# Local and downsampled attention with a gated MLP on one core: the opening's order planned anew

## The chip, the core and the metric

The kernel runs on one core of one Trainium2 chip. The core has a matrix engine (PE, with its weight loads beside it), a vector engine (DVE), a scalar engine (ACT), GpSimd (POOL) and a queue engine (SP). Each takes its instructions in order. Transfers are issued from SP, ACT and POOL. The metric is the device time of one execution in microseconds (us); less is better.

## The reference

Eight batches, eight heads, 576 positions, 64 numbers a head. The attention output is a coarse attention over means of four positions, repeated four times, plus a local attention in which a position sees those at a distance under four. The result, as 4608 tokens of 512, goes through an RMS norm and a gated MLP of width 1536.

```python
q_d, k_d, v_d = (t.reshape(B, H, S // 4, 4, D).mean(axis=3) for t in (q, k, v))
out_up = np.repeat(sm_attn(q_d, k_d, v_d), 4, axis=2)
mask = np.abs(pos[:, None] - pos[None, :]) < 4
scores = np.where(mask, scale * np.matmul(q, k.transpose(0, 1, 3, 2)), -1e9)
x = out_up + np.matmul(softmax(scores), v)         # then tokens x 512
xn = x / np.sqrt(np.mean(x * x, axis=-1, keepdims=True) + 1e-06) * rms_g
g, val = xn @ w_gate, xn @ w_val
return (g * (1.0 / (1.0 + np.exp(-g))) * val) @ w_out
```

## The kernel before

The tokens are cut into 18 chunks of 256. A chunk's MLP (class `Forward`) has six steps `n`: a gate and a value product of the first layer (`first`, L1388; x and weights are each split into a high and a low half, three matmuls for one product), the gating on ACT and DVE (`tanh`, `gate`, `product`, `high`, L1396 to L1410), the low half of the gated product (`low`, L1413, on DVE or POOL), and the second layer (`second`, L1427), which runs a step behind.

The x of a chunk comes from local attention. From chunk 2 on, class `Attention` makes it on DVE (scores L917 and L921, sums of values L980), with a part of the value products on ACT (L963) and, for chunks 2 and 3, on POOL (L970); then come the squares, the mean across partitions (L1010), an inverse root by three Newton steps (L718 to L731), the norm, and a turn of x on PE (L1033) into the halves `xh` and `xl` (L1037, L1041). Chunks 0 and 1 are made by class `Early` with matmuls instead: four scores for each of two units (`score`, L1166 for the band mask and L1168 for the products, on 64 rows each), their maxima (L1181), a scaling of the maxima (`less`, L1185), exponentials (L1192), an inverse sum (L1198, L1199), turns (L1227, L1238), the values (L1258), the coarse result spread over four positions (`spread`, L1265), a copy (`keep`, L703 is the line of all copies), squares (L1278) and a turn (L1303).

The coarse attention (class `Coarse`) runs for a batch and a pair of heads: scores (L593), maxima (L603), their scaling (L608), exponentials (L613), turns (L623), values (L638), an inverse sum (L644, L647), a scaled result (L656) that goes out to memory (L659). Its sums over four positions are made for batch 0 on DVE (L473, L481; class `OpeningSums`, which also puts the queries in order on ACT, L467) and later by accumulating transfers from POOL (L417).

The weights arrive as 64-bit floats and are decoded in 20 pieces (`load_weight`, `decode`): a scaling on ACT (L315), the last bits on POOL (L325), a join on DVE (L332), a high half on ACT (L339) and a low half on DVE (L346, L344). The first layer's halves are multiplied by the norm's gain `g_sb`, which `load_small` fetches from POOL's queue (L1535) with the edge masks (L1534).

Until chunk 3 the order of all this is written out by a planner at build time (class `Plan`). Each step is a task with an engine (or a choice of two), a cost in us, a due time and the buffers that it takes and uses; a transfer has a size times `MB` us, and a table `RANK` holds one due time for every task. The planner goes through time, gives each free engine the task with the earliest due time of those that can start first, and calls it; the instructions stand on each engine in that order (`manual_schedule`) as long as a task's planned start is before `due[FIRST] + 10`. After that the same calls are made, and the framework's own scheduler orders them; from chunk 3 a hand-written interleaving (`steps`) follows.

`heat` fills PE's planned idle time with matmuls on constants (L504), so that the clock stays up. In the opening they go into a spare PSUM tile of the pool `ps_o`, which has two buffers; the two units of chunk 0 use that pool for their values, and the spare is closed as the second of them begins (`value`).

Of the kernel before, what the change touches and what calls it, by code (L numbers as in the profile page):

```python
# [19 lines left out]
P = 128  # L20
# [31 lines left out]
WARM_AT = 6.5  # L52
WARM_SHARE = 0.95
WARM_LEAST = 0.4
MB = 3.1
# [72 lines left out]
class Plan:  # L128
# [9 lines left out]
    def add(self, engine, cost, fn, due, after=(), with_=(), allocs=(), uses=(), not_before=0.0, dma=0.0, lag=0.0, hw=0, sw=0):  # L138
# [45 lines left out]
    def run(self, until=1e9):  # L184
        free, ready = self.free, self.ready
        while self.left:
# [19 lines left out]
            if s >= until:  # L206
                return
            cost = next(o for o in t.options if o[0] == e)[1]
            t.start = s
            self.idle, self.gap = (s - max(known, WARM_AT), s - max(free[e], WARM_AT)) if e == "PE" else (0.0, 0.0)  # L210
# [20 lines left out]
def attn_moe_kernel(  # L231
# [25 lines left out]
    ps_o = ctx.enter_context(tc.tile_pool(name="ps_o", bufs=2, space=PSUM))  # L257
# [99 lines left out]
    def load_second(f, m):  # L357
# [9 lines left out]
        "up_t": 2, "xh0": 1, "xh1": 1, "xl0": 1, "xl1": 1, "sil": 2, "hs": 2, "o_sb": W_BUFS, "ps_h": 3, "ps_o": 2, "ps_a": 3,  # L367
# [60 lines left out]
    class OpeningSums:  # L428


        def __init__(self, b, half):
            self.b, self.half = b, half
            self.qk_buf, self.vs_buf, self.q_buf = buf("qk"), buf("vs"), buf("hs")
            self.got = task("SP", 0.4, self.load_qk, -100 + half, dma=1.18 * MB, hw=1)
# [1220 lines left out]
```

## Time and profile before

| | us |
|---|---|
| median of three runs | 1089.92 (1088.96 to 1090.8) |
| the profiled execution | 1089.94 |
| its span, first to last instruction | 1088.1 |
| PE busy | 1066.7 (98%) |
| PE weight load busy | 970.2 (89%) |
| DVE busy | 909.6 (84%) |
| ACT busy | 598.6 (55%) |
| POOL busy | 160.8 (15%) |
| first-layer matmuls (L1388), both forms | 632.6 + 482.5 |
| second-layer matmuls (L1427) | 327.1 |

Busy times of matmuls overlap, so that those of single groups add up to more than the engine's. A matmul of the filler counts as busy as well. A row of a group gives line, engine, operation, output and inputs by the program's names, shapes and count, then busy us and mean ns of one, then the idle time of the engine just before them and what ended most of it. A row of a timeline gives start, duration, engine, line and operation, and in brackets the idle time before it with what ended it. The releaser is inferred: where the engine named had long been done, it was another.

### The profile page before, as it was taken

The numbers are of one execution on the slowest core, as the hardware profiler recorded it, in microseconds if no ns is written. First come the engines' busy times: TensorE is split into PE (matmuls) and PEld (weight loads), VectorE is DVE, ScalarE is ACT, GpSimd is POOL, SyncE is SP. The second block draws the span as 40 slices with busy tenths as digits, with TensorE's granted clock in tenths as the row PEclk, the third lists the DMA queues.
The fourth block names the chain that finished last, engine by engine and source line by source line (L and its number), as shares of the span: only waits on it lengthen the run. The fifth ranks groups of instructions, "written<-read, shape, count | busy, mean of one in ns | idle before, by whom it ended". The sixth has DMA issues, their size and how long they took to land.

```text
span 1088.1 us, 21642 instructions
## 1 busy us (share of the span) xinstructions
PE 1066.7 (98%) x7983; PEld 970.2 (89%) x7983; DVE 909.6 (84%) x1554; ACT 598.6 (55%) x2029; POOL 160.8 (15%) x200
## 2 busy tenths in 40 slices
PE   7899999999999999999999999999999999999997
PEld 4569899899989999999999999999999999999996
DVE  7799999798969897979797979798998898986421
ACT  4686565737266565656564737383737373645111
POOL 6544564300210101010101010100000000000000
PEclk9899999999999999999999999999999999999999
DMA  9885657333654535353525253522221222210000
GB/s 292 274 237 167 182 134 155 77 91 86 132 102 117 118 99 102 107 106 87 126 85 128 68 130 86 132 77 82 63 86 54 79 78 74 80 40 20 1 20 20
DMA packets 79182, 114.09 MB, mean 105 GB/s; under 512 B 33038, under 2 KB 40406, under 8 KB 79076
## 3 DMA queue, kind: packets, MB, share of 16 engines
q1 hardware_dynamic: 48308, 88.40, 26.3%
q0 software_dynamic: 11680, 19.78, 11.6%
q10 hardware_dynamic: 19088, 4.53, 1.9%
q8 instruction: 62, 1.02, 0.4%
q14 instruction: 44, 0.36, 0.1%
HBM read 100.86 MB, written 11.80 MB: 104 GB/s over the span
## 4 chain that ended last, share of the span: by engine, by line
PE 85%; DVE 6%; DMA 3%; issue 2%; POOL 2%; ACT 1%; SPq 1%; DVEq 0%; POOLq 0%; ACTq 0%
PE ps_h L1388 51%; PE ps_o L1427 25%; PE ps_a L638 3%; DMA w<-in_w_val_dram 1%; PE ps_a L593 1%; PE ps_a L623 1%; DVE prod L917 1%; PE ps_a L1033 1%; DVE x_t L980 1%; DVE sc L921 1%; PE ps_a L1258 1%; DVE sil L1404 0%; POOL hs L1413 0%; DMA vs<-in_v_sum_dram 0%; DMA wo<-in_w_val_dram 0%
## 5 line engine op out<-in xcount | busy, mean ns | idle before, releaser
L1388 PE MATMUL ps_h<-xh,w 128*128 128x256 f32 x3456 | 632.6, 281 | 0.0
L1388 PEld LDWEIGHTS ps_h<-xh,w 128*128 128x128 f32 x3456 | 537.6, 188 | 9.7 <-issue 3.1
L1388 PE MATMUL ps_h<-xl,w 128*128 128x256 f32 x1728 | 482.5, 280 | 0.0
L1427 PE MATMUL ps_o<-wo,hs 128*128 128x512 f32 x1296 | 327.1, 396 | 4.2 <-POOL hs L1413 1.7
L1388 PEld LDWEIGHTS ps_h<-xl,w 128*128 128x128 f32 x1728 | 325.2, 188 | 5.8 <-issue 2.0
L963 ACT ACTIVATE prod<-kv,sc 128x64 f32<-128x64 f32 x1024 | 261.9, 406 | 28.9 <-DVE sc L954 15.5
L1427 PEld LDWEIGHTS ps_o<-wo,hs 128*128 128x128 f32 x1296 | 232.8, 188 | 49.1 <-DVE hs L1413 2.8
L980 DVE TENSOR_REDUCE x_t<-prod 128x128 f32<-128x896 f32 x128 | 134.5, 1080 | 39.5 <-PE ps_a L1033 36.8
L1410 ACT ACTIVATE hs<-sil 128x512 fp32r<-128x512 f32 x108 | 68.2, 631 | 165.5 <-DVE sil L1404 140.1
L1396 ACT ACTIVATE sil<-ps_h 128x512 f32<-128x512 f32 x108 | 64.1, 595 | 148.7 <-PE ps_h L1388 140.8
L917 DVE TENSOR_TENSOR prod<-q_t,kv 128x896 f32<-128x896 f32 x128 | 138.6, 1089 | 0.2
L921 DVE TENSOR_REDUCE sc<-prod 128x14 f32<-128x896 f32 x128 | 136.9, 1075 | 0.2
L1399 DVE SCALAR_TENSOR_TENSOR sil<-sil,ps_h 128x512 f32<-128x512 f32 x108 | 73.7, 683 | 52.1 <-ACT sil L1396 52.1
L970 DVE TENSOR_TENSOR prod<-sc,kv 128x384 f32<-128x384 f32 (+1 forms) x128 | 105.9, 868 | 0.1
L1404 DVE SCALAR_TENSOR_TENSOR sil<-sil,ps_h 128x512 f32<-128x512 f32 x108 | 73.9, 684 | 22.6 <-PE ps_h L1388 22.1
L417 POOL DMA_DIRECT2D qk<-in_qk_sum_dram x42 | 39.0, 928 | 340.0 <-DMA qk<-in_qk_sum_dram 282.1
L1413 DVE TENSOR_TENSOR hs<-sil,hs 128x512 fp32r<-128x512 f32 x102 | 69.9, 685 | 17.9 <-ACT hs L1410 17.8
L613 ACT ACTIVATE a_g<-ps_a,m_g 72x144 f32<-72x144 f32 x128 | 46.5, 370 | 54.2 <-DVE m_g L608 50.0
L417 POOL DMA_DIRECT2D vs<-in_v_sum_dram x42 | 39.4, 937 | 104.1 <-DMA vs<-in_v_sum_dram 80.7
L1003 ACT ACTIVATE up_t<-x_t 128x128 f32<-128x128 f32 x128 | 39.1, 305 | 18.3 <-DVE x_t L993 12.2
L638 PEld LDWEIGHTS ps_a<-vs,a_g 72*72 72x72 f32 x512 | 39.2, 150 | 7.4 <-ACT a_g L613 2.9
L638 PE MATMUL ps_a<-vs,a_g 72*72 72x64 f32 x512 | 40.8, 234 | 5.1 <-ACT a_g L613 2.7
(154 smaller groups left out, 808.0 us busy)
## 6 DMA issues: line engine op xcount, KB each, us to landing
kv<-in_k_pad_dram SPq DMA_DIRECT2D x56, 320.0 KB
kv<-in_v_pad_dram SPq DMA_DIRECT2D x56, 320.0 KB
qk<-in_qk_sum_dram POOLq DMA_DIRECT2D x42, 288.0 KB, 4.5
out_dram<-o_sb SPq DMA_DIRECT2D x96, 72.0 KB
vs<-in_v_sum_dram POOLq DMA_DIRECT2D x42, 144.0 KB, 4.3
q_t<-in_q_band_dram SPq DMA_DIRECT2D x150, 36.0 KB
w<-in_w_gate_dram SPq DMA_DIRECT2D x8, 512.0 KB
w<-in_w_val_dram SPq DMA_DIRECT2D x8, 512.0 KB
```

The source lines that it names most:

```text
L417: nc.gpsimd.dma_start(out=t, in_=(qk_sum, v_sum)[i][self.b, j, :, self.half], accum_op=ALU.add)
L638: nc.tensor.matmul(out=op[:, par, c], lhsT=at[:, kc, c * HALF:(c + 1) * HALF], rhs=self.sums.vs[:, 2 * (self.hp % 2) + par, kc], start=(kc ...
L917: nc.vector.tensor_tensor(out=pr, in0=bcast(q[:, s0:s0 + 2], 2, NO), in1=window(k, s0), op=ALU.mult)
L921: nc.vector.tensor_reduce(out=self.sc[:, j, par, s0:s0 + 2], in_=self.pr[i], axis=AX.X, op=ALU.add,)
L963: nc.scalar.activation(out=self.pr[i][:, o, s], in_=self.v[j, par][:, s0 + s + o], func=AF.Copy, scale=p[:, s, o:o + 1],)
L970: (nc.vector if engine == "DVE" else nc.gpsimd).tensor_tensor(out=self.pr[i][:, a:b], in0=bcast(p[:, :, a:b].rearrange("p s o -> p o s"), ...
L980: nc.vector.tensor_reduce(out=self.x[j][:, s0:s0 + 2, par], in_=pr.rearrange("p o s d -> p s d o"), axis=AX.X, op=ALU.add,)
L1388: self.last = nc.tensor.matmul(out=p[n][:, i], lhsT=wi[:, k], rhs=xi[:, k], start=(m == 0), stop=(m == 3 * KT - 1),).ins
L1399: nc.vector.scalar_tensor_tensor(out=self.sil[n], in0=self.sil[n], scalar=1.0, in1=self.g[n], op0=ALU.add, op1=ALU.mult,)
L1404: nc.vector.scalar_tensor_tensor(out=self.sil[n], in0=self.sil[n], scalar=0.5, in1=self.v[n], op0=ALU.mult, op1=ALU.mult,)
L1413: (nc.gpsimd if engine == "POOL" else nc.vector).tensor_tensor(out=self.hs[n][:, 1], in0=self.sil[n], in1=self.hs[n][:, 0], op=ALU.subtract,)
L1427: nc.tensor.matmul(out=self.o[j], lhsT=lhs[:, cols], rhs=rhs, start=(f == 0 and m == 0), stop=(f == NF - 1 and m == 2),)
```

## The change

All costs of the tasks are measured anew (some 30 of them: `MB` is 2.7 for 3.1, the opening's value loads are 1.2 MB for 0.26), and the planner learns two things. Until `COLD` = 11.5 us a PE task costs twice as much and half as many fillers are issued. And a DVE task with `port=True` does not start while a computing POOL task runs, nor the reverse. `RANK` is a new table. The fixed order lasts until chunk 3's x is turned.

```diff
-WARM_AT = 6.5
+WARM_AT = 5.5
+COLD = 11.5
+PORT = {"DVE": "POOL", "POOL": "DVE"}
-MB = 3.1
+MB = 2.7
...
+        t.port = ({"DVE"} if port else set()) | (set() if sw else {"POOL"})
...
-                        found.append((max(free[e], t.at, at, floor), t, max(free[e], at)))
+                        s = max(free[e], t.at, at, floor)
+                        if e in t.port:
+                            a, b = self.held[PORT[e]]
+                            s = b if a <= s < b else s
+                        found.append((s, t, max(free[e], at)))
...
-            cost = next(o for o in t.options if o[0] == e)[1]
+            cost = next(o for o in t.options if o[0] == e)[1] * (2 if e == "PE" and s < COLD else 1)
...
-        plan.run(due[FIRST] + 10)
+        plan.run(atts[FIRST].turned)
```

The queries are ordered with a factor of -0.125 and the mask has the other sign, so that the scores of chunks 0 and 1 come out negated and scaled: their minimum is used as it stands, and the scaling of the maxima (L1185) goes. Two scores of a pair of heads become one task, in which the two 64-row halves alternate.

```diff
-            nc.scalar.copy(out=self.q, in_=raw)
+            nc.scalar.activation(out=self.q, in_=raw, func=AF.Copy, scale=-0.125)
...
+            for n in pair:
+                nc.tensor.matmul(
+                    out=self.s[u, n], lhsT=one_sb, rhs=bcast(near_sb[:, FAC * (1 - lo):FAC * (1 - lo + NEAR_K)], 1, 2),
+                    start=True, stop=False,
+                )
             for h in range(2):
+                for par, n in enumerate(pair):
+                    rows = slice(par * D, (par + 1) * D)
+                    nc.tensor.matmul(
+                        out=self.s[u, n][:, h].rearrange("p (n j) -> p j n", j=FAC), lhsT=q[rows, h, FAC * n0:FAC * (n0 + GRP)],
+                        rhs=k[rows, h, :, n0 - lo:n0 - lo + NEAR_K], start=False, stop=(h == 1),
+                    )
...
-            nc.vector.tensor_reduce(out=self.heads(self.m[u], n), in_=self.s[u, n], axis=AX.X, op=ALU.max)
+            nc.vector.tensor_reduce(out=self.heads(self.m[u], n), in_=self.s[u, n], axis=AX.X, op=ALU.min)
```

In the planned part, the scaling of the coarse maxima (L608) and the addition before the inverse sum (L644, and L1198 of chunks 0 and 1) move from DVE to ACT as tasks of their own (`scale`, `more`, 0.2 us each in the plan). The last bits of a weight may go to ACT instead of POOL.

```diff
-            scale = task("DVE", 0.16, self.scale, at, peaks, uses=[m])
+            scale = task("ACT", 0.2, lambda: self.scale("ACT"), at, peaks, uses=[m])
...
-            inv = task("DVE", 0.33, self.invert, at, exps, uses=[z])
+            more = task("ACT", 0.2, lambda: self.more("ACT"), at, exps, uses=[z])
+            inv = task("DVE", 0.2, self.invert, at, [more], uses=[z])
...
+        def more(self, u):
+            nc.scalar.activation(out=self.z[u], in_=self.z[u], func=AF.Copy, bias=1e-9)
...
-        bits = task("POOL", (0.75, 1.55)[m - 1], lambda: last_bits("POOL"), at, [got], uses=[raw])
+        bits = task(
+            (("POOL", (0.68, 1.13)[m - 1], at), ("ACT", (0.6, 1.03)[m - 1], at + 12)), 0, last_bits, at, [got], uses=[raw],
+        )
```

The pool `ps_o` gets two tiles of one buffer each. The filler holds `ps_o0` from the start until chunk 0's x is turned; both units of chunk 0 use `ps_o1`, one after the other. The gain vector is fetched from ACT's queue as the second instruction there.

```diff
+    def open_spare():
+        spare.update(open=True, tile=ps_o.tile([P, DM], FP32, name="ps_o0"))
+
+    def close_spare():
+        heat(spare["tile"])
+        spare["open"] = False
...
+    nc.scalar.dma_start(out=g_sb, in_=rms_g)
...
-        nc.gpsimd.dma_start(out=g_sb, in_=rms_g)
...
-        Early(0).plan(X_DUE[0], (ps_h, "ps_h"), (ps_o, "ps_o")),
+        Early(0).plan(X_DUE[0], (ps_h, "ps_h"), (ps_o, "ps_o1")),
...
+    spare_buf = buf("ps_o0")
+    task("PE", 0.01, open_spare, -999, allocs=[spare_buf])
+    task("PE", 0.01, close_spare, due[0], atts[0].turns, uses=[spare_buf])
```

More of the change, by code (lines that the diff above doesn't have):

```diff
@@ L136, in buf, with add @@
         return Buf(res)
-    def add(self, engine, cost, fn, due, after=(), with_=(), allocs=(), uses=(), not_before=0.0, dma=0.0, lag=0.0, hw=0, sw=0):
+    def add(self, engine, cost, fn, due, after=(), with_=(), allocs=(), uses=(), not_before=0.0, dma=0.0, lag=0.0, hw=0, sw=0, port=False):
         options = [(engine, cost, due)] if isinstance(engine, str) else list(engine)
@@ L182, in open, with run @@
             self.ready[e].append(t)
-    def run(self, until=1e9):
+    def run(self, last=()):
         free, ready = self.free, self.ready
-        while self.left:
+        while self.left and not (last and all(t.start is not None for t in last)):
             best = None
@@ L366, in attn_moe_kernel @@
         "qk": 2, "vs": 2, "a_g": 4, "o_g": 2, "m_g": 2, "z_g": 2, "kv": 4, "q_t": 2, "prod": 2, "sc": 2, "x_t": 2,
-        "up_t": 2, "xh0": 1, "xh1": 1, "xl0": 1, "xl1": 1, "sil": 2, "hs": 2, "o_sb": W_BUFS, "ps_h": 3, "ps_o": 2, "ps_a": 3,
+        "up_t": 2, "xh0": 1, "xh1": 1, "xl0": 1, "xl1": 1, "sil": 2, "hs": 2, "o_sb": W_BUFS, "ps_h": 3, "ps_o0": 1, "ps_o1": 1, "ps_a": 3,
         "hw": 8, "sw": 8, "rms": 1, **{f"first{i}": 1 for i in range(4)}, **{f"second{i}": 1 for i in range(2)},
@@ L439, in __init__ @@
                 add = task(
-                    "DVE", 0.7, lambda j=j: self.add(j), at, [add], allocs=[self.qk_buf] if j == 1 else [], uses=[self.qk_buf],
+                    "DVE", 0.75, lambda j=j: self.add(j), at, [add], allocs=[self.qk_buf] if j == 1 else [], uses=[self.qk_buf], port=True,
                 )
@@ L447, in __init__ @@
                 last = task(
-                    (("POOL", 1.34, at + 10), ("DVE", 0.62, at + 10)), 0, lambda e, j=j: self.add_v(j, e), at, [last],
-                    allocs=[self.vs_buf] if j == 1 else [], uses=[self.vs_buf],
+                    (("POOL", 1.25, at + 10), ("DVE", 0.65, at + 10)), 0, lambda e, j=j: self.add_v(j, e), at, [last],
+                    allocs=[self.vs_buf] if j == 1 else [], uses=[self.vs_buf], port=True,
                 )
@@ L492, in heat @@
         if spare["open"] and made:
-            if "tile" not in spare:
-                spare["tile"] = ps_o.tile([P, DM], FP32, name="ps_o")
             out, fresh, n = spare["tile"], True, plan.gap
-        n, plan.idle, plan.gap = n * WARM_SHARE, 0.0, 0.0
+        n, plan.idle, plan.gap = n * plan.share, 0.0, 0.0
         cols = 1
@@ L531, in high @@
             def high():
+                self.more()
                 self.invert()
@@ L605, in attn_moe_kernel, with scale @@
         SC = 1.0 / (FAC * FAC * 8.0)
-        def scale(self):
-            nc.vector.tensor_scalar(out=self.m, in0=self.m, scalar1=-self.SC, scalar2=None, op0=ALU.mult)
+        def scale(self, engine="DVE"):
+            if engine == "ACT":
+                nc.scalar.activation(out=self.m, in_=self.m, func=AF.Copy, scale=-self.SC)
+            else:
+                nc.vector.tensor_scalar(out=self.m, in0=self.m, scalar1=-self.SC, scalar2=None, op0=ALU.mult)
         def powers(self, par):
@@ L641, in values, with more @@
                         )
+        def more(self, engine="DVE"):
+            if engine == "ACT":
+                nc.scalar.activation(out=self.z, in_=self.z, func=AF.Copy, scale=float(FAC), bias=FAC * 1e-9)
+            else:
+                nc.vector.tensor_scalar(
+                    out=self.z, in0=self.z, scalar1=1e-9, scalar2=float(FAC), op0=ALU.add, op1=ALU.mult,
+                )
         def invert(self):
-            nc.vector.tensor_scalar(
-                out=self.z, in0=self.z, scalar1=1e-9, scalar2=float(FAC), op0=ALU.add, op1=ALU.mult,
-            )
             nc.vector.reciprocal(out=self.z, in_=self.z)
@@ L866, in plan @@
                 add = task(
-                    "DVE", 0.69, lambda j=j: self.add_up(j), T - 18 + 3 * j, [made[4 * j + 3], load],
-                    uses=[ups[j], xs[j]],
+                    "DVE", 0.62, lambda j=j: self.add_up(j), T - 18 + 3 * j, [made[4 * j + 3], load],
+                    uses=[ups[j], xs[j]], port=True,
                 )
@@ L878, in plan @@
             for j in range(2):
-                norm = task("DVE", 0.69, lambda j=j: self.norm(j), T - 8, [root], uses=[xs[j]])
+                norm = task("DVE", 0.62, lambda j=j: self.norm(j), T - 8, [root], uses=[xs[j]], port=True)
                 turn = task(
@@ L1066, in plan @@
                 sps = [buf(self.s_tag) for _ in range(4)]
-                for n in range(4):
+                for half in range(2):
+                    pair = (2 * half, 2 * half + 1)
                     score = task(
-                        "PE", 0.8, lambda u=u, n=n: self.score(u, n), at - TAIL,
-                        [sums[0, n // 2].q_got, near_got[0], one_got, *(used["qk"][-1:] if n % 2 else [])],
-                        allocs=sps[n:n + 2] if n % 2 == 0 else [], uses=[sps[n], sums[0, n // 2].q_buf],
+                        "PE", 1.15, lambda u=u, half=half: self.scores(u, half), at - TAIL, [sums[0, half].q_got, near_got[0], one_got],
+                        allocs=[sps[n] for n in pair], uses=[*[sps[n] for n in pair], sums[0, half].q_buf],
@@ L1082, in plan @@
-                inv = task("DVE", 0.33, lambda u=u: self.invert(u), at, powers)
+                    for n in pair:
+                        scored[n] = task("DVE", 0.42, lambda u=u, n=n: self.peak(u, n), at, [score], uses=[sps[n]])
+                powers = [
+                    task("ACT", 0.62, lambda u=u, n=n: self.powers(u, n), at, [scored[n]], uses=[sps[n]]) for n in range(4)
+                ]
+                more = task("ACT", 0.2, lambda u=u: self.more(u), at, powers)
+                inv = task("DVE", 0.2, lambda u=u: self.invert(u), at, [more])
@@ L1110, in plan @@
                 used["x"].append(keep)
-                squares.append(task("ACT", 0.8, lambda u=u: self.squares(u), at, [keep], uses=[y]))
+                squares.append(task("ACT", 0.6, lambda u=u: self.squares(u), at, [keep], uses=[y]))
             rms = task("DVE", 0.5, self.rms, T - 6, squares, allocs=[r])
-            root = task("DVE", 1.65, self.root, T - 6, [rms], uses=[r])
+            root = task("DVE", 1.7, self.root, T - 6, [rms], uses=[r], port=True)
             self.turned, turns = [], []
@@ L1116, in plan @@
                 norm = task(
-                    (("ACT", 0.7, T - 4), ("DVE", 0.45, T - 3.9)), 0, lambda e, u=u: self.norm(u, e), T - 4, [root], uses=[xs[j]],
+                    (("ACT", 0.65, T - 4), ("DVE", 0.42, T - 3.9)), 0, lambda e, u=u: self.norm(u, e), T - 4, [root], uses=[xs[j]], port=True,
                 )
@@ L1244, in value @@
         def value(self, u):
-            if self.y_tag == "ps_o" and (self.y or "tile" not in spare):
-                if "tile" in spare:
-                    heat(spare["tile"])
-                spare["open"] = False
             y = self.y[u] = self.y_pool.tile([P, DM], FP32, name=self.y_tag)
@@ L1342, in plan @@
             att, c, T = self.att, self.c, due[self.c]
-            o_bufs = [buf("ps_o") for _ in range(2)]
+            o_bufs = [buf(f"ps_o{j}") for j in range(2)]
             last = None
@@ L1365, in plan @@
                 low = task(
-                    (("DVE", 0.6, soon), ("POOL", 1.55, soon)), 0, lambda e, n=n: self.low(n, e), soon, [high], uses=[sil, hs],
+                    (("DVE", 0.6, soon), ("POOL", 1.3, soon)), 0, lambda e, n=n: self.low(n, e), soon, [high], uses=[sil, hs], port=True,
                 )
@@ L1419, in second @@
             if f == 0:
-                self.o = [ps_o.tile([P, DM], FP32, name="ps_o") for _ in range(2)]
+                self.o = [ps_o.tile([P, DM], FP32, name=f"ps_o{j}") for j in range(2)]
             heat(self.o[0], fresh=f == 0)
@@ L1482, in decode @@
         scaled = task("ACT", (0.6, 1.03)[m - 1], scale, at, [got], uses=[raw])
-        join_ = task("DVE", (0.62, 1.15)[m - 1], join, at, [scaled, bits], uses=[raw])
+        join_ = task("DVE", (0.62, 1.15)[m - 1], join, at, [scaled, bits], uses=[raw], port=True)
         hi = task("ACT", (0.62, 1.1)[m - 1], high, at, [join_, *own], uses=[raw])
-        low = task("DVE", (0.64, 1.2)[m - 1], split, at, [hi], uses=[raw])
+        low = task("DVE", (0.64, 1.2)[m - 1], split, at, [hi], uses=[raw], port=True)
         whole.append(low)
```

92 lines of the change are left out of this document (38 added, 54 removed), and 94 rows, old and new, of the table RANK.

## The prediction

> **What bounds the kernel now.** I read the windows of the engines first (stretch in us; then length, busy us and instructions of PE, weight load, DVE, ACT, POOL; then granted clock, DMA share, GB/s), with the span above them, and then the same windows for the warming matmuls of line 504 alone (PE, weight load, clock, DMA, GB/s).
>
> ```profile
> core 0: 1088.1 us, clock 0.992
> 0.00:78.50 78.50, 67.95 (x386) 42.84 (x387) 63.03 (x122) 52.39 (x142) 42.23 (x53) 0.91 0.87 275
> 78.50:204.00 125.50, 122.94 (x940) 110.97 (x939) 117.77 (x195) 79.19 (x225) 62.64 (x74) 1.00 0.61 147
> 204.00:300.00 96.00, 96.00 (x745) 89.44 (x744) 84.42 (x129) 49.90 (x185) 13.65 (x25) 1.00 0.40 101
> 345.00:1081.00 736.00, 736.00 (x5579) 687.65 (x5578) 607.88 (x1041) 384.93 (x1357) 36.34 (x42) 1.00 0.32 80
> ```
>
> ```profile
> 0.00:78.50 78.50, 24.65 (x80) 8.71 (x80) 0.91 0.87 275
> 78.50:204.00 125.50, 3.41 (x21) 2.00 (x20) 1.00 0.61 147
> ```
>
> Three stages. From 345 us to 1081 the PE never pauses: nothing here can change but by starting earlier. From 78.5 to 204 it loses 125.5 - 122.94 = 2.56 us idle and 3.41 us to filler, 6.0 in all, while DVE is busy for 117.77 of 125.5. Before 78.5 it does little of use: of 67.95 busy, 24.65 are filler. The feed-forward work begins here (timeline of the PE):
>
> ```profile
> 78.22 0.47 PE L1388 MATMUL ps_h<-xh,w 128*128 128x256 f32 x1
> ```
>
> So the time is that start, plus a fixed amount of PE work, plus about 6 us lost in the next stage. The change can pay by an earlier start and by fewer losses up to 204; both must hold, because an earlier start makes the PE want chunk 2's x earlier from a DVE with 7.7 us to spare. The profiled execution took 1089.94 us (span 1088.1 and 1.8 around it); the median shown is 1089.92, so a difference against the one is a difference against the other.
>
> **Term 1: the gain vector.** These are rows of the timelines of POOL, ACT, DVE and PE, then the issue's row (KB, us to landing).
>
> ```profile
> 27.75 1.27 POOL L481 TENSOR_TENSOR vs<-vs,w 72x512 f32<-72x512 f32 x1 [2.16 <-DVE vs L481]
> 31.52 0.58 POOL L1535 DMA_DIRECT2D g_sb<-in_rms_g_dram  x1
> 36.38 1.21 ACT L339 ACTIVATE w<-w,g_sb 128x1024 fp32r<-128x1024 f32 x1 [6.01 <-POOL w L325]
> 31.63 0.17 DVE L608 TENSOR_SCALAR m_g<-m_g 72x4 f32<-72x4 f32 x1
> 38.36 1.22 PE L638 MATMUL ps_a<-vs,a_g 72*72 72x64 f32 x8 [2.71 <-ACT a_g L613]
> 40.53 1.22 PE L638 MATMUL ps_a<-vs,a_g 72*72 72x64 f32 x8 [0.95 <-DVE a_g L705]
> g_sb<-in_rms_g_dram POOLq DMA_DIRECT2D x1, 2.0 KB, 4.8
> ```
>
> The first split of a first-layer weight (L339) needs g_sb. That load is issued on POOL at 31.52 and lands 4.8 later, at 36.3; ACT starts L339 at 36.38. The row names POOL's L325 as releaser, but g_sb is what came last. ACT had been idle since 36.38 - 6.01 = 30.4, and the value sums whose room the weight takes were done at 29.0. ACT therefore stood 6.01 us with the exponentials of the coarse attention queued behind, and PE waited for those (2.71). The change issues g_sb on ACT's queue before everything. What is late next is L608, done at 31.8: the exponentials could run then, instead of behind L339, which ends at 37.6. **-5.6** (bounds 0, if the new order parks ACT elsewhere, and -6.0).
>
> **Term 2: the cold clock behind that wait.** Windows of the PE (busy, clock), and of its fillers (PE, weight load, clock):
>
> ```profile
> 40.50:48.00 7.50, 7.47 (x45) 0.53 0.60 203
> 40.50:48.00 7.50, 1.49 (x3) 0.45 (x3) 0.53 0.60 203
> ```
>
> After the two pauses the PE ran 7.47 - 1.49 = 5.98 us of useful work at a clock of 0.53; at full clock that is 3.2. **-2.8** (bounds 0 and -2.8); the longer filler window and the doubled cold costs in the planner serve the same end. The Trainium skill, "TensorE: Matmul & The Clock Gate", section "What's actually happening", says that the clock halves after an idle window of about 3.4 us and returns after one busy window of that length; by it half of 3.4, or 1.7, would be lost here. The row shows the half rate for over 7 us, so the measurement decides.
>
> **Term 3: pairs of scores.** Before, a unit's scores run one 64-row group after the other; after, the two halves alternate as the coarse scores (L593) already do. From the chain of waits (first and last of the four on it between 50 and 78.5) and the PE's timeline:
>
> ```profile
> 53.66 0.69 PE ps_h L1168 x4
> ...
> 75.35 0.69 PE ps_h L1168 x4
> 50.05 0.71 PE L593 MATMUL ps_a<-qk 64*72 64x144 f32 x8
> 53.59 0.76 PE L1168 MATMUL ps_h<-w,hs 64*128 64x136 f32 x4
> ```
>
> Alternated, eight matmuls of about the same width take 0.71 where four take 0.76. Half of four pieces of 0.69 leaves the chain: **-1.4** (bounds 0, if PSUM keeps them apart, and -1.4). The other pairs stand beside filler and give nothing.
>
> **Term 4: DVE's small operations.** Groups of DVE, 0 to 200 us, and the one row of 800 to 1000 us, where POOL computes nothing, ahead of the last two:
>
> ```profile
> L1185 DVE TENSOR_SCALAR m_e<-m_e 128x4 f32<-128x4 f32 x8 | 3.5, 443 | 0.2
> L608 DVE TENSOR_SCALAR m_g<-m_g 72x4 f32<-72x4 f32 x10 | 2.4, 236 | 0.2
> L644 DVE TENSOR_SCALAR z_g<-z_g 72x4 f32<-72x4 f32 x10 | 5.7, 568 | 1.6 <-ACT a_g L613 1.6
> L1198 DVE TENSOR_SCALAR z_e<-z_e 128x8 f32<-128x8 f32 x4 | 1.7, 436 | 0.7 <-ACT w L1192 0.7
> L644 DVE TENSOR_SCALAR z_g<-z_g 72x4 f32<-72x4 f32 x1 | 0.2, 172 | 0.0
> 56.04 0.91 DVE L1185 TENSOR_SCALAR m_e<-m_e 128x4 f32<-128x4 f32 x1
> 70.00 1.07 DVE L729 SCALAR_TENSOR_TENSOR newton<-rinv 128x2 f32<-128x2 f32 x1
> ```
>
> Prescaled, negated queries remove L1185; L608, L644 and L1198 go to ACT. That is 3.5 + 2.4 + 5.7 + 1.7 = 13.3 us off DVE by 204. L644 costs 568 ns on average beside a busy POOL and 172 alone, so some 4 of those 13.3 were waits. On the chain before 78.5, L1185's 0.91 goes, and L729's 1.07 would shrink by 0.9 if it no longer meets POOL: **-1.8** (bounds -0.9 and -1.8).
>
> The Trainium skill, "SBUF — State Buffer", section "Who interferes with whom", calls the pair of ports that DVE and GpSimd share an exclusive lock for a whole instruction. By it, planning around the lock makes no time: one of the two engines still stands still, and term 4 would be the removed 0.9 alone and the sum 0.9 higher, inside the forecast's own range. The trace agrees as far as 568 against 172 goes.
>
> **Terms 5 and 6: what is added.** Chunk 0's two units now share one PSUM tile (ps_o1), while the filler keeps the other. From the timelines and, for the values, the chain:
>
> ```profile
> 59.99 0.41 DVE L656 TENSOR_TENSOR xl<-ps_a,z_g 72x256 f32<-72x256 f32 x1
> 61.79 1.94 PE L1265 MATMUL ps_o<-xl,wo 72*128 72x512 f32 x4
> 63.38 0.60 ACT L703 COPY x_t<-ps_o 128x512 f32<-128x512 f32 x1
> 65.50 0.60 ACT L1278 ACTIVATE ps_o<-ps_o 128x512 f32<-128x512 f32 x1
> 66.61 0.21 ACT L1278 ACTIVATION_READ_ACCUMULATOR ps_o<-ps_o 128x1 f32 x1
> 50.76 2.78 PE ps_o L1258 x18
> ```
>
> Before, the last coarse result is out at 60.4 and both units' squares end at 66.8, 6.4 later. With one tile, the second unit's values wait for the first's squares: half of 1.94 for its spread, 0.60 copy, 0.60 + 0.21 squares, then 2.78 values, and spread, copy, squares again: 7.5, and with five handovers of about 0.25 some 8.9. **+2.5** (bounds 0, if the first unit ends ahead of the last coarse head, and +2.5). On PE the wait is filled; behind it on ACT stand weight steps.
>
> ACT receives 12 scalings, 12 + 4 additions: 28 small operations, 12 of them before 78.5. The nearest row and ACT's load there:
>
> ```profile
> 2.50 0.21 ACT L1495 ACTIVATE zero_sb<-zero_sb 128x16 bf16<-128x16 bf16 x1
> 50.00:78.50 28.50, 28.10 (x180) 19.02 (x180) 26.37 (x54) 25.00 (x68) 12.79 (x11) 1.00 0.84 259
> ```
>
> 12 x 0.21 = 2.5 us on an engine with 3.5 free in that window: **+1.0** (bounds 0 and +2.5); once ACT has no room it is all of it.
>
> Start: -5.6 - 2.8 - 1.4 - 1.8 + 2.5 + 1.0 = -8.1, so about 70.
>
> **The next stage.** With the start 8 earlier, DVE must be 8 earlier with chunk 2's x. It sheds 13.3 and its idle wait for L339, 3.2. I take 2 of the 6.0 lost there as recovered (bounds +1, for handovers planned in the wrong order, and -6.0); much of the rest hangs on the low half of the gated product, which POOL makes in 1820 ns and DVE in 685 (groups up to 200 us and of the page; the last row is the turn of chunk 2's x):
>
> ```profile
> L1413 POOL TENSOR_TENSOR hs<-sil,hs 128x512 fp32r<-128x512 f32 x6 | 10.9, 1820 | 15.9 <-ACT hs L1410 15.9
> L1413 DVE TENSOR_TENSOR hs<-sil,hs 128x512 fp32r<-128x512 f32 x102 | 69.9, 685 | 17.9 <-ACT hs L1410 17.8
> 198.29 0.60 PE L1033 MATMUL ps_a<-ident_sb,x_t 128*128 128x128 f32 x4
> ```
>
> These may return to DVE under the port rule, 6 x 0.685 = 4.1, which still leaves 9 of the relief. Weight bits that may move from POOL to ACT, recalibrated costs and the fixed order up to chunk 3's x instead of a due time change only order; I price them at nothing, covered by the full PE of 204 to 300. Without that cover, a late x costs its lateness. Sum: 1089.9 - 8.1 - 2 = 1079.8, **1080**.
>
> **Rivals.** *All of it*: the first unit is early (term 5 at 0), ACT has room (0), all 6.0 come back: -11.6 - 6.0 = -17.6, **1072**. For: DVE's relief of 13.3 plus 3.2 just carries it. Against: nothing else may slip. 0.14.
>
> *Hidden*: the start moves, but chunk 2's x does not. If the low halves return to DVE (4.1) and the queued order uses 5 more for weights, 13.3 leaves about 4; with the mean of the squares and POOL's queue in between I take 3: **1087**. For: DVE's 117.77 of 125.5. Against: the PE has second-layer work of chunk 1 to put in. That the pairs do not overlap or the lock waits reappear falls here. 0.23.
>
> *Slower*: the planned loads are late and a decode again parks ACT ahead of chunk 0's chain. The planner now books 2.7 us per MB; the transfers of 0 to 40 us:
>
> ```profile
> DMA packets 8808, 11.98 MB, mean 300 GB/s; under 512 B 5268, under 2 KB 5460, under 8 KB 8805
> ```
>
> 300 GB/s is 3.3 us per MB, 0.6 more; after the 8.8 MB that the first group needs (sums 2 x 1.18 and 2 x 0.59, values 4 x 0.26, weights 8 x 0.52, by their shapes) that is 5.3 late. Then terms 1 and 2 return in another place: -8.1 + 5.6 + 2.8 + 5.3 = +5.6, **1095.5**. It decides once a decode is queued ahead of the exponentials by more than the 8.4 us of terms 1 and 2. Against: value loads are booked at 1.2 MB, not 0.26, which adds about 10 us of planned transfer. 0.15.
>
> **Numbers.** Forecast 0.48 (1075 to 1085), all 0.14, hidden 0.23, slower 0.15. A measurement here can tell about 0.2%, 2.2 us: hidden lies at that edge, 0.13 of it faster and 0.10 same. Faster 0.75, same 0.10, slower 0.15. The range leaves out the slower case and the tail of the best: 1070 to 1091.
>
> **What would show it.** g_sb lands before 10 us and no ACT idle near 6 us ahead of L339 (term 1); clock at 1.00 from 20 us on (2); a pair of scores at about 0.75 (3); no L1185, small ACT rows of 0.2 (4, 6); the second unit's values behind the first's squares (5); first L1388 near 70; filler and idle after it near 4. I am wrong if the start stays above 76, or if chunk 2's x, turned at 198 before, is not turned by 190.

## The result, and the profile after

The changed kernel takes **1106.77 us** (1104.27 to 1107.54), the kernel before in the same runs 1090.36: a ratio of **1.0142** (95% interval 1.0124 to 1.016), by which it is some 15.5 us slower. One of its four executions took 1321.1 us, at a granted clock of 0.746: the median counts it, the range and the ratio do not. The forecast was 1080 and the range 1070 to 1091. The profile read here is of one more execution of the unaltered changed kernel (1107.44 us, span 1105.7).

First the windows of the engines, as in the prediction, then those of the filler alone (L518 now), then the first matmul of the first layer (L1407 now):

```profile
core 0: 1105.7 us, clock 0.982
0.00:78.50 78.50, 61.05 (x391) 37.00 (x392) 59.80 (x107) 56.59 (x159) 38.10 (x49) 0.89 0.79 252
78.50:204.00 125.50, 114.17 (x854) 103.23 (x854) 100.86 (x152) 71.31 (x208) 64.47 (x74) 0.95 0.64 154
204.00:300.00 96.00, 92.42 (x680) 84.89 (x680) 82.51 (x135) 55.26 (x200) 13.68 (x16) 0.96 0.35 89
300.00:345.00 45.00, 45.00 (x352) 41.17 (x351) 33.34 (x66) 21.84 (x79) 8.51 (x10) 1.00 0.58 113
345.00:1098.50 753.50, 753.50 (x5718) 704.19 (x5717) 625.23 (x1066) 398.50 (x1416) 36.26 (x42) 1.00 0.32 81
```

```profile
0.00:78.50 78.50, 22.73 (x82) 8.15 (x82) 0.89 0.79 252
204.00:300.00 96.00, 5.57 (x28) 4.43 (x28) 0.96 0.35 89
```

```profile
77.90 0.47 PE L1407 MATMUL ps_h<-xh,w 128*128 128x256 f32 x1
```

The one row of before that the comparison still lacks:

```profile
300.00:345.00 45.00, 43.02 (x341) 38.95 (x340) 36.49 (x72) 31.03 (x122) 5.99 (x7) 1.00 0.46 103
```

Two things are to be seen. The first layer starts at 77.90 where it started at 78.22: **the opening gained nothing**. And from there to 345 the PE now stands 125.5 - 114.17 + 96 - 92.42 = 14.9 us where it stood 2.56 + 45 - 43.02 = 4.5. The span's 17.6 us divide so: start -0.3, idle +10.4, filler 5.57 for about 4.1, +1.4. The rest, about 6, was not measured apart; the clock of 0.95 and 0.96, where it was 1.00, is enough for it (0.05 of 114.17 and 0.04 of 92.42 busy us make 9.4, an estimate). After 345 the PE never pauses, as before. The longest waits of the PE between 78 and 345 (engine, line, releaser: us in total, times, longest), after and then before:

```profile
PE ps_o L1446 <- POOL hs L1432: 4.8, 2, 3.2
PE ps_a L609 <- DMA qk<-in_qk_sum_dram: 3.4, 2, 3.1
PE ps_a L657 <- DVE a_g L729: 2.7, 1, 2.7
PE ps_a L1057 <- DVE x_t L1044: 1.9, 1, 1.9
PE ps_a L518 <- DVE xl L1065: 1.2, 1, 1.2
```

```profile
PE ps_o L1427 <- POOL hs L1413: 1.7, 2, 1.4
PE ps_o L1427 <- DVE hs L1413: 1.5, 2, 0.8
PE ps_o L1427 <- ACT hs L1410: 0.8, 1, 0.8
```

The low halves that POOL makes (L1432) and the coarse sums that POOL's queue adds up by DMA (read by L609) lead the list.

**What ate the start.** Timelines of the changed kernel: DVE, ACT's queue, POOL, SP, PE, and the PE's window behind it.

```profile
23.47 0.42 DVE L680 TENSOR_TENSOR xl<-ps_a,z_g 72x256 f32<-72x256 f32 x1
```

```profile
24.21 0.42 ACT L727 COPY a_g<-ps_a 72x288 f32<-72x288 f32 x1
32.16 0.57 ACTq L683 DMA_DIRECT2D up<-xl  x1
32.83 1.13 ACT L324 ACTIVATE w<-w 128x1024 f32<-128x1024 f32 x1 [8.20 <-DMA up<-xl]
```

```profile
32.16 1.27 POOL L490 TENSOR_TENSOR vs<-w 72x512 f32<-72x512 f32 x1 [3.74 <-DMA w<-in_v_sum_dram]
```

```profile
19.74 0.40 SPq L471 DMA_DIRECT2D w<-in_v_sum_dram  x1
```

```profile
34.71 0.38 PE L1186 MATMUL ps_h<-near_sb,one_sb 128*128 128x272 bf16 x1 [5.47 <-ACT w L1213]
```

```profile
34.50:37.00 2.50, 2.29 (x11) 1.25 (x11) 1.43 (x3) 2.50 (x16) 1.10 (x1) 0.50 1.03 407
```

ACT stands for 8.20 us in front of the store of the first coarse head (L683), with the exponentials L1213 queued behind it, and the PE then stands 5.47. The store's data were ready at 23.9 (L680). It starts at 32.16, in the same instant as POOL's L490, which waits for nothing but the second load of value sums (L471) to land. The lists of waits in the built program say why. In it each DMA of the queues of SP and ACT raises one of eight semaphores (the expectations call them lanes), given out in turn over both queues, and a semaphore's next user must wait until its last one has landed. L471 is the 13th DMA of SP and the 15th of the two queues, the store the 23rd:

```
SP   13  L471 DMA w<-in_v_sum_dram    [waits DMAHW6]
ACT      L683 DMA up<-xl              [waits DMAHW6, DVE]
```

The store is a whole round of eight behind L471 and so waits for that load. This load was issued at 4.64 us before the change and is issued at 19.74 after it; before, the store's semaphore was that of a value load issued at 18.65, and ACT stood 0.6 us there.

### The profile page after: what moved, and what is told of

The parts are those of the page before. It is cut to its first block, busy times and chain, and to the rows that moved or that the text cites. A ratio compares the mean times of both kernels' runs of the same rounds, so it can differ in the third digit from the quotient of the medians.

```text
span 1319.3 us, 21630 instructions
## 1 busy us (share of the span) xinstructions
PE 1295.3 (98%) x7988; PEld 1140.0 (86%) x7988; DVE 909.1 (69%) x1523; ACT 611.7 (46%) x2059; POOL 157.7 (12%) x189
## 4 chain that ended last, share of the span: by engine, by line
PE 95%; DMA 2%; SPq 1%; DVE 1%; issue 0%; POOL 0%; ACT 0%; ACTq 0%; POOLq 0%; DVEq 0%
PE ps_h L1407 56%; PE ps_o L1446 27%; PE ps_a L657 3%; PE ps_a L609 2%; PE ps_a L642 1%; PE ps_a L1057 1%; PE ps_o L518 1%; DMA w<-in_v_sum_dram 1%; SPq L318 1%; DMA qk<-in_qk_sum_dram 1%; PE ps_a L1277 1%; PE ps_o L1277 1%; PE ps_a L518 0%; PE ps_a L1250 0%; PE ps_h L518 0%
## 5 line engine op out<-in xcount | busy, mean ns | idle before, releaser
L1407 PE MATMUL ps_h<-xh,w 128*128 128x256 f32 x3456 | 771.2, 316 | 0.0
L1407 PEld LDWEIGHTS ps_h<-xh,w 128*128 128x128 f32 x3456 | 630.2, 216 | 17.4 <-issue 5.4
L1407 PE MATMUL ps_h<-xl,w 128*128 128x256 f32 x1728 | 543.7, 315 | 0.0
L1446 PE MATMUL ps_o<-wo,hs 128*128 128x512 f32 x1296 | 397.6, 459 | 1.4 <-POOL hs L1432 1.4
L1407 PEld LDWEIGHTS ps_h<-xl,w 128*128 128x128 f32 x1728 | 373.5, 216 | 10.7 <-issue 2.4
L1446 PEld LDWEIGHTS ps_o<-wo,hs 128*128 128x128 f32 x1296 | 251.7, 204 | 82.2 <-POOL hs L1432 1.9
L426 POOL DMA_DIRECT2D qk<-in_qk_sum_dram x42 | 39.7, 944 | 411.1 <-DMA qk<-in_qk_sum_dram 279.1
L1432 DVE TENSOR_TENSOR hs<-sil,hs 128x512 fp32r<-128x512 f32 x100 | 70.0, 700 | 25.2 <-ACT hs L1429 24.6
L632 ACT ACTIVATE a_g<-ps_a,m_g 72x144 f32<-72x144 f32 x128 | 46.5, 371 | 24.2 <-DVE m_g L627 17.9
L426 POOL DMA_DIRECT2D vs<-in_v_sum_dram x42 | 36.2, 861 | 124.4 <-DMA vs<-in_v_sum_dram 115.1
L727 ACT COPY a_g<-ps_a 72x288 f32<-72x288 f32 x59 | 23.0, 394 | 54.2 <-PE ps_a L642 51.3
L619 DVE TENSOR_REDUCE m_g<-ps_a 72x2 f32<-72x288 f32 x64 | 26.3, 448 | 30.3 <-PE ps_a L609 30.3
L657 PEld LDWEIGHTS ps_a<-vs,a_g 72*72 72x72 f32 x512 | 45.8, 170 | 1.6 <-issue 0.5
```

What stands on the lines that cost most here:

```text
L426: nc.gpsimd.dma_start(out=t, in_=(qk_sum, v_sum)[i][self.b, j, :, self.half], accum_op=ALU.add)
L657: nc.tensor.matmul(out=op[:, par, c], lhsT=at[:, kc, c * HALF:(c + 1) * HALF], rhs=self.sums.vs[:, 2 * (self.hp % 2) + par, kc], start=(kc ...
L1407: self.last = nc.tensor.matmul(out=p[n][:, i], lhsT=wi[:, k], rhs=xi[:, k], start=(m == 0), stop=(m == 3 * KT - 1),).ins
L1432: (nc.gpsimd if engine == "POOL" else nc.vector).tensor_tensor(out=self.hs[n][:, 1], in0=self.sil[n], in1=self.hs[n][:, 0], op=ALU.subtract,)
L1446: nc.tensor.matmul(out=self.o[j], lhsT=lhs[:, cols], rhs=rhs, start=(f == 0 and m == 0), stop=(f == NF - 1 and m == 2),)
```

## The experiments

Start is that of the first layer; idle and filler are those of the PE from there on, worked out up to 345 us from each profile's windows as above; the ratio is to the kernel before on the same chip. Different jobs are compared by their ratios, 0.001 being 1.1 us.

| run | start | idle | filler | median us | ratio (95%) |
|---|---|---|---|---|---|
| before | 78.2 | 4.5 | 4 | 1089.92 | 1 |
| changed | 77.9 | 14.9 | 5.6 | 1106.77 | 1.0142 (1.0124 to 1.016) |
| after_stores | 68.4 | 15.3 | 5.6 | 1096.76 | 1.0044 (1.0023 to 1.0065) |
| before_g | 76.8 | 4.8 | 4 | 1090.32 | 0.9989 (0.9971 to 1.0007) |
| stores_gpool | 68.3 | 15.6 | 3.4 | 1097.52 | 1.006 (1.0038 to 1.0081) |
| stores_until | 66.9 | 16.6 | 3.4 | 1098.99 | 1.0079 (1.0054 to 1.0105) |
| stores_nofill | 68.3 | 13.1 | 0 | 1094.1 | 1.0027 (1.0008 to 1.0046) |
| stores_low | 67.7 | 7.9 | 4.7 | 1091.25 | 1.0002 (0.998 to 1.0024) |
| nofill_low | 71.3 | 9.1 | 0 | 1088.39 | 0.9965 (0.9943 to 0.9986) |
| nofill_sums | 66.8 | 8.4 | 0 | 1083.05 | 0.9938 (0.9915 to 0.9962) |
| before_low_nofill | 78.4 | 5.4 | 0 | 1090.29 | 0.9981 (0.9967 to 0.9996) |
| before_sums | 80.9 | 3.1 | 4 | 1090.7 | 0.999 (0.9977 to 1.0003) |
| parked_low_nofill | 74.7 | 11 | 0 | 1094.37 | 1.0032 (1.0016 to 1.0049) |

A start is that of one execution. Up to the first layer, stores_nofill and nofill_low have the same order, and their starts lie 3.0 us apart, at granted clocks of 0.83 and 0.62 from 20 to 30 us; before and before_sums lie 2.7 apart, at 0.85 and 0.74 from 20 to 40 us. So starts that differ by 3 us or less show nothing.

**after_again** is the unaltered changed kernel, whose profile is the one above.

> The changed kernel unaltered, for a profile at full clock (the first one had a granted clock of 0.746). Both theories: 1104 to 1108 us. In the lane theory ACT stands 8 us ahead of the first store of a coarse head, PE 6 to 7 us behind it, and the first L1407 comes later than the 78.2 us of before, by about the whole difference of 15 us. In the theory of the next stage the first L1407 stays at 70 to 80 us and PE idles between there and 250 us.

Each theory came in part. ACT stands 8.20 us ahead of the store and the PE 5.47, as in the first; the first layer is not later than before, and the PE stands 14.9 us behind it, as in the second.

**after_stores**: is the semaphore's wait what ate the start? The stores of batch 0's first three coarse heads go out with the fourth's.

```diff
-    whole_og = {}
+    whole_og, late_store = {}, []
...
-            nc.scalar.dma_start(out=up_dram[self.b][self.hp]..., in_=self.og)
+            if not self.b:
+                late_store.append(self)
+                if len(late_store) < KT:
+                    return
+            for x in late_store if not self.b else [self]:
+                nc.scalar.dma_start(out=up_dram[x.b][x.hp]..., in_=x.og)
```

> The stores of the first three coarse heads of batch 0 are issued together with the fourth's, so that no store stands in ACT's queue before 45 us. Lane theory (the first store waits for the DMA lane of a value-sum load that lands at 31 us, and ACT, PE and the clock stand behind it): 6 to 10 us less than the changed kernel, 1096 to 1100 us, ACT's wait of 8 us gone. Rival (what stands behind the store is late anyway, or the fillers fill the time): within 2 us of the changed kernel, 1104 to 1108 us.

The first layer, and the windows of 20 to 40 us of this run and of the kernel before:

```profile
68.36 0.47 PE L1412 MATMUL ps_h<-xh,w 128*128 128x256 f32 x1
20.00:40.00 20.00, 18.66 (x182) 14.01 (x183) 18.13 (x35) 18.63 (x77) 13.03 (x13) 1.00 1.02 332
```

```profile
20.00:40.00 20.00, 15.62 (x92) 9.29 (x91) 15.36 (x29) 9.18 (x35) 14.00 (x16) 0.85 0.97 309
```

ACT no longer stands; from 20 to 40 us it is busy for 18.63 us against 9.18 before the change, and the clock is 1.00 against 0.85. The first layer starts 9.5 us earlier and the kernel gains 0.0098, 10.7 us, a little more than the 6 to 10 expected. So the wait cost about two thirds of what the change lost. But with a start 9.9 us ahead of before, the run is still slower than before: the 15.3 us of idle have not moved.

**before_g**: the term with the highest price in the prediction, alone. The kernel before, with only the load of the gain vector on ACT's queue.

```diff
     nc.scalar.dma_start(out=ident_sb, in_=ident)
+    nc.scalar.dma_start(out=g_sb, in_=rms_g)
...
-        nc.gpsimd.dma_start(out=g_sb, in_=rms_g)
```

> The kernel before with the gain vector loaded from ACT's queue as its second instruction, and nothing else of the change. By terms 1 and 2 of the prediction: 8 us less than before, 1082 us, ACT's 6 us ahead of L339 gone and the clock at 1.00 between 40 and 48 us. Rival (one more load on the hardware lanes moves the waits of the loads behind it, and another wait takes the place): 1089 to 1095 us.

ACT's timeline, the PE's, then a piece of the chain of waits (start, us, what), and the same load in the chain of the kernel before:

```profile
30.57 1.20 ACT L339 ACTIVATE w<-w,g_sb 128x1024 fp32r<-128x1024 f32 x1
```

```profile
76.79 0.47 PE L1388 MATMUL ps_h<-xh,w 128*128 128x256 f32 x1
```

```profile
54.61 2.07 DVE wo L344
57.11 5.25 DMA wo<-in_w_val_dram
62.36 0.69 DVE wo L1219
```

```profile
60.51 4.82 DMA wo<-in_w_val_dram
```

And the window of 40 to 60 us of before_g (DVE is the third busy number):

```profile
40.00:60.00 20.00, 19.70 (x152) 14.29 (x152) 19.75 (x31) 17.45 (x50) 7.59 (x6) 1.00 0.80 274
```

The wait of 6.01 us is gone and L339 runs 5.8 us earlier. Of the 8.4 us that terms 1 and 2 put on that, 3.4 are left when DVE's splits (L344) free the room for the next weight, whose load is issued at 57.1 instead of 60.5, and 1.4 at the first layer, less than the scatter of the starts. The time did not measurably change: 1090.32 us, as the rival expected.

**stores_gpool**: the same load, put back on POOL's queue in after_stores (the diff above, reversed).

> The kernel of after_stores with the gain vector loaded from POOL again, as before the change. In after_stores the first split that needs it (L348) runs at 35.6 us; a load among POOL's small ones, issued near 24, would land near 31. Theory A (the prediction's: moving this load is worth 5.6 to 8.4 us of the start): first layer from 68.4 back to 74 or later, and the run 5 to 8 us slower than after_stores. Theory B (the new order puts the first split late enough that the load's queue does not matter): start within 2 us of 68.4, time within 2 us of after_stores.

The split's row in the two runs, first stores_gpool (first and last start in it):

```profile
L348 ACT ACTIVATE w<-w,g_sb x8: 1227/1244/1277, 35.8 to 71.1; 128x1024 fp32r<-128x1024 f32 x8
```

```profile
L348 ACT ACTIVATE w<-w,g_sb x8: 1240/1248/1296, 35.6 to 71.2; 128x1024 fp32r<-128x1024 f32 x8
```

Theory B. The start is 68.27 against 68.36, the ratios' intervals overlap. In the new order the first split comes at 35.6 anyway, and a load from POOL is in time.

**stores_until**: is the new end of the fixed order the later loss?

```diff
-        plan.run(atts[FIRST].turned)
+        plan.run(until=due[FIRST] + 10)
```

> The kernel of the run after_stores, with one thing undone: the fixed order ends at the planned time due[FIRST]+10, as before the change, and not when chunk 3's x is turned. In after_stores the first layer of chunk 3 starts at 269.9 us behind 3.15 us of PE idle and 21 fillers of 4.64 us, that themselves start only when x is ready. Theory A (the new end of the fixed order makes this hole): the run is 5 to 8 us faster than after_stores (1096.8), about 1090, and PE has under 2 us of idle and filler between 245 and 275. Theory B (x is late because loads and POOL's parked queue made it late, wherever the fixed order ends): within 2 us of 1096.8, the hole only moves.

Theory B: 1098.99 us, no gain (2.2 us above after_stores, with overlapping intervals). The pauses in front of chunk 3 shrink from 3.15 us to 1.9, but 1.5 come back at 326, where the kernel before has the same 1.5.

**stores_nofill**: after_stores with no filler once chunk 0's x is turned.

```diff
-        spare["open"] = False
+        spare.update(open=False, closed=True)
...
+        if spare.get("closed"):
+            return
         n = plan.idle
```

> The kernel of after_stores without any filler once chunk 0's x is turned (28 matmuls on zeros go, 5.6 us by the windows). Theory A (the 21 fillers at 265 start after x is ready and so stand on the path in full): 4 to 5.5 us faster than after_stores, about 1092. Theory B (they cover a wait that is there anyway): no change, 1096 to 1097, with 4.6 us of idle in their place; colder clock behind it could make it 1 us slower.

In after_stores the PE's timeline reads

```profile
265.24 4.64 PE L518 MATMUL ps_a<-zero_sb,one_sb 128*72 128x256 bf16 x21 [1.24 <-DVE xl L1070]
269.53 0.56 PE L1412 MATMUL ps_h<-xl,w 128*128 128x256 f32 x1
```

The fillers wait for xl themselves, and the first layer comes behind them: they fill a hole that is over. Without them the first layer starts as soon as xl is there. The median gains 0.0017, 1.9 us, with overlapping intervals. That is less than the 4 to 5.5 us of theory A and more than the nothing of theory B; the size stays open.

**nofill_low** and **stores_low**: the low halves that the plan gives to POOL run on DVE, without the fillers and with them.

```diff
-            (nc.gpsimd if engine == "POOL" else nc.vector).tensor_tensor(
+            nc.vector.tensor_tensor(
                 out=self.hs[n][:, 1], in0=self.sil[n], in1=self.hs[n][:, 0], op=ALU.subtract,
```

> The kernel of stores_nofill, with the low halves of the gated product that the plan puts on POOL computed on DVE instead. In after_stores PE waits 4.49 us at 186 for such a half, because POOL stands parked in an accumulating load with the half behind it; DVE has 27 us idle from 140 to 262. Theory A (POOL's parked queue is on the path): 3 to 5 us faster than stores_nofill. Theory B (what PE wants next is late by as much, or DVE pays its 0.68 us each on the path): within 1.5 us of stores_nofill.

> The kernel of after_stores with the low halves that the plan puts on POOL computed on DVE, fillers kept. It separates the two edits of nofill_low. Theory A (POOL's parked queue costs its 4.5 us by itself): 4 to 6 us faster than after_stores, ratio to the kernel before 0.999 to 1.001. Theory B (the edits only work together): within 2 us of after_stores, ratio 1.002 or more.

What it takes away, in after_stores (timelines of the PE and of POOL's queue):

```profile
191.10 1.22 PE L1451 MATMUL ps_o<-wo,hs 128*128 128x512 f32 x2 [4.49 <-POOL hs L1437]
```

```profile
90.00 0.84 POOL L426 DMA_DIRECT2D vs<-in_v_sum_dram  x1 [5.56 <-DMA vs<-in_v_sum_dram]
94.92 1.00 POOL L426 DMA_DIRECT2D qk<-in_qk_sum_dram  x1
188.89 0.86 POOL L426 DMA_DIRECT2D qk<-in_qk_sum_dram  x1 [3.93 <-DMA qk<-in_qk_sum_dram]
189.47 1.57 POOL L1437 TENSOR_TENSOR hs<-sil,hs 128x512 fp32r<-128x512 f32 x1
```

POOL works its queue in order. Each adding load (L426) waits until the one before it on the same sum has landed, as the built program lists it, and what is queued behind stands too. The low half at 189.47 is such a case: ACT had done its high half (L1434) at 181.8, the load ahead of it stood 3.93 us, and the PE goes on as the low half ends. On DVE the low halves cost 0.68 us each, and the PE waits for none of them: stores_low is 0.0042 faster than after_stores (4.6 us; the intervals just touch), nofill_low 0.0062 faster than stores_nofill (6.8 us). Theory A in both, somewhat above its number in the second. **nofill_low is faster than both kernels**, 0.9965 of before.

**nofill_sums**: do the sums' loads land late because of their bytes? Each adding load of batches 1 to 7 adds only half of its columns; the rest of the added parts is left out of the coarse sums.

```diff
-            nc.gpsimd.dma_start(out=t, in_=(qk_sum, v_sum)[i][self.b, j, :, self.half], accum_op=ALU.add)
+            n = t.shape[1] // 2
+            nc.gpsimd.dma_start(out=t[:, :n], in_=(qk_sum, v_sum)[i][self.b, j, :, self.half][:, :n], accum_op=ALU.add)
```

> The kernel of stores_nofill, where each accumulating load of the coarse sums of batches 1 to 7 adds only the first half of its columns (the rest of the three added parts is left out of the sums). That halves 17.3 of the 19.8 MB on POOL's queue. In after_stores PE waits 5.09 us at 94.5 for the first such sum. Theory A (those sums land late, planned at 3.4 us where they take 4.4 to 8.2): that wait falls under 1.5 us, and the run is 4 to 8 us faster than stores_nofill. Theory B (the landing time is set by the issue behind other queued work, not by the bytes): the wait stays above 3 us and the gain is under 2 us.

The wait for the first sum is under 0.2 us (5.09 in after_stores, 1.27 in the profile of stores_nofill), that for POOL's low half falls from 4.75 to 1.28. The medians differ by 11 us (0.0089 in the ratios), the two profiled spans by 7.9 (1088.0 to 1080.1): theory A, at its upper end or above. The first score on a sum, which stands 5.09 us in after_stores, waits for the last of that sum's three additions. This is issued at 94.92 (row above), when the PE already stands, and lies in POOL's queue behind the addition at 90.00 that stood 5.56. Whether fewer bytes help by landing sooner themselves or by leaving room to other loads was not told apart.

**before_sums**, its control: the same edit in the kernel before.

> The kernel before the change, where each accumulating load of the coarse sums of batches 1 to 7 adds only the first half of its columns (the rest of the three added parts is left out), as in nofill_sums. Theory A (before the change these sums had cover, since the first layer began at 78 and the first score on them was wanted at 111): within 3 us of before, ratio 0.997 to 1.001. Theory B (their bytes are on the path in any order): 7 us faster or more, ratio 0.993 or less, as nofill_sums stands to stores_nofill (0.991).

Theory A: 0.999, no measurable change. The late sums are a cost of the new order alone. Rows of SP and PE, from the first load of batch 1's sums to the first score on them: the kernel before, the changed kernel, after_stores:

```profile
66.09 0.56 SPq L413 DMA_DIRECT2D vs<-in_v_sum_dram  x1
111.20 0.71 PE L593 MATMUL ps_a<-qk 64*72 64x144 f32 x8
```

```profile
76.54 0.43 SPq L422 DMA_DIRECT2D vs<-in_v_sum_dram  x1
107.16 1.24 PE L609 MATMUL ps_a<-qk 64*72 64x144 f32 x8 [3.13 <-DMA qk<-in_qk_sum_dram]
```

```profile
66.83 0.44 SPq L422 DMA_DIRECT2D vs<-in_v_sum_dram  x1
99.58 1.24 PE L609 MATMUL ps_a<-qk 64*72 64x144 f32 x8 [5.09 <-DMA qk<-in_qk_sum_dram]
```

Before, 45 us lie between load and score. In the changed kernel the score stands in the PE's queue from 104.0 on, 27 us behind the load; in after_stores from 94.5 on, 28 us. The changed kernel's first layer starts when it did before, so an earlier start is not what took the cover. Counted from the first layer, the new order issues the load 10.8 us later and wants the score 6.9 us sooner.

**before_low_nofill**: the two edits of nofill_low in the kernel before.

> The kernel before the change with the same two edits as nofill_low: low halves on DVE alone, no filler once the first layer has begun (4.0 us go). Its PE waits for POOL's low halves only 1.36 and 0.38 us after 78. Theory A (the changed kernel's POOL queue made that wait, and before had cover): 1 to 4 us faster than before, ratio 0.996 to 0.999, so nofill_low (0.9965) keeps no clear lead over it. Theory B (the edits are as good there as in the changed kernel): 6 to 8 us faster, ratio about 0.993. Theory C (DVE, busy 158 of 171 us from 78 to 249 there, has no room): slower than before.

Theory A, at its lower end: 0.9981. Its interval overlaps that of nofill_low, so the mended new opening has no clear lead over the old one with the same two edits.

**parked_low_nofill**: nofill_low with the stores where the change has them.

> The changed kernel with the two edits of nofill_low (low halves on DVE, no filler once chunk 0's x is turned), but with its stores where the change has them, so that ACT stands again for the store's lane. Theory A (the parked ACT and the later losses are separate): first layer near 78, and 8 to 11 us slower than nofill_low, ratio to before 1.004 to 1.007. Theory B (with a later start the loads are in time, so the two losses overlap): 3 to 6 us slower than nofill_low, ratio 0.999 to 1.002.

Between the two. The first layer starts at 74.7 and the run is 0.0067 (7.3 us) slower than nofill_low, where the same stores cost 10.7 us in the changed kernel. From the changed kernel, moving the stores gains 0.0098, the other two edits 0.0110, and all of them 0.0177, which is 0.0031 less than the sum. So the two losses are mostly separate; an overlap of 0.0031 is less than these intervals can tell.

## Why the prediction was wrong

**Terms 1 and 2 (-5.6 and -2.8)** failed first. The mechanism was read rightly: the load was late, ACT stood, and before_g removes it. But a wait of 6 us on the chain was booked in full at the first layer, 40 us later, with an engine in between (DVE, busy for 19.75 of the 20 us from 40 to 60) that had no room to come sooner. At most 1.4 us arrive. (The size was also off by a little: by its own rows, 37.6 - 31.8, the term is 5.8.) In the new order with its stores moved, the load's queue makes no difference at all (stores_gpool). Its own lower bound, "0, if the new order parks ACT elsewhere", was what happened: 8.20 us at the store. I had looked for a decode as the place of that wait, and never at whom a store's semaphore waits for.

**Term 3** was read rightly in its mechanism, and **term 4** and **term 6** in their row sizes: eight alternating scores take 0.77, the small operations on ACT take 0.19, L1185 is gone, and of the Newton steps, one of which took 1.07, none takes over 0.18. Rows of PE, ACT and DVE (the last: shortest, median, longest ns):

```profile
44.29 0.77 PE L1193 MATMUL ps_h<-w,hs 64*128 64x136 f32 x8
34.57 0.19 ACT L625 ACTIVATE m_g<-m_g 72x4 f32<-72x4 f32 x1
L753 DVE SCALAR_TENSOR_TENSOR newton<-rinv x54: 103/161/181, 67.0 to 1025.3; 128x8 f32<-128x8 f32 x48, 128x2 f32<-128x2 f32 x6
```

Their shares of the start, and **term 5**'s, were not measured apart.

**The start, "about 70"**, is 77.9, and 68.4 once the store is out of the way. So the sum of -8.1 came near the 9.9 us that are then gained, but by luck: its largest terms were not what made it, as the moved load gives nothing. The new order keeps ACT at work where it stood; which of its edits does so was not taken apart.

**"The next stage -2"** is the step that cost most: from the first layer to the end the kernel lost 17.9. I saw that an earlier start needs chunk 2's x from DVE earlier, and took DVE's 13.3 us of relief for the answer. But DVE is idle for 25 of the 125.5 us now; what is late comes through POOL's queue, the sums' additions and the low halves behind them, and those were not looked at. The sum took the stage after the first layer to run as before and 2 us better; the new order left the first of these sums 27 us from load to score, where it had 45. Chunk 2's x is turned at 210.6 (198.3 before, and 190 was my own mark for being wrong).

**"I price them at nothing, covered by the full PE of 204 to 300"**: the fixed order's end shows no cost by itself (stores_until), but the cover is gone, with 3.58 us of idle and 5.57 of filler in that window.

**The slower rival** (1095.5, given 0.15) named both things that happened, late loads and a parked ACT. It had the wrong place for the second, and its 5.3 us of late loads lay in the opening, not in the stage after it. It was too small by 11 us and had too small a chance. The *hidden* rival's mechanism, a start that moves while the next stage does not, is what after_stores shows; there the next stage even gives back more than the start gained.

What stays open: how much of the sums' lateness is the planner's rate (2.7 us per MB) and how much the order it chose. No order planned at another rate was run.

## What to carry to other kernels

A wait that ends at the start of a chain is worth only what is left of it at that chain's end: follow it past the next engine that has no idle time before booking it. When a stage starts earlier or is ordered anew, list every load that it wants, and compare how long each lies between issue and use in the old order and in the new; that slack is what covers its landing. On an engine that works its queue in order, look at what each DMA issue in it may wait for, its semaphore's last user included, and keep work that others wait for out from behind it.

## What the runs showed of the hardware

A pause of the PE costs more than its length here. After the pause of 5.09 us in after_stores the windows of the PE read

```profile
99.50:102.00 2.50, 2.42 (x11) 1.85 (x12) 2.50 (x4) 0.00 (x0) 1.12 (x3) 0.50 0.60 75
102.00:104.50 2.50, 2.50 (x9) 1.93 (x9) 2.47 (x5) 1.43 (x3) 2.30 (x5) 0.70 0.90 207
104.50:107.00 2.50, 2.40 (x21) 1.96 (x20) 2.50 (x3) 2.35 (x11) 2.07 (x3) 1.00 1.03 353
```

Half the clock for 2.5 us and 0.70 for as long again lose 2.5 x 0.5 + 2.5 x 0.3 = 2.0 us of work (an estimate), and no idle row shows them. The Trainium skill, "TensorE: Matmul & The Clock Gate", section "What's actually happening", says that the clock halves after an idle window of about 3.4 us and returns after a busy window of that length; this pause agrees. In front of chunk 3 such a length is not reached: two pauses of 1.91 and 1.24 us lie 6 us apart, and around the second and behind it the windows read

```profile
262.00:266.00 4.00, 2.37 (x14) 1.67 (x13) 4.00 (x8) 4.00 (x17) 0.86 (x1) 0.74 0.53 153
266.00:270.00 4.00, 4.00 (x21) 3.42 (x20) 3.93 (x6) 3.60 (x18) 0.00 (x0) 0.50 0.56 124
```

There the clock is 0.50 for 4 us while the PE is busy, the fillers among it, with 1.63 us of idle in the window ahead. Narrower windows read 0.99 from 262 to 264 us and 0.50 from there on, so the half clock is there as the second pause begins; what set it is not shown.
